# Decode attention with an MLP gate: one program loop over single units, with the small matrices behind the last one

## The chip, the cores and the metric

One core of a Trainium2 chip. The metric is the device time in microseconds of one execution. The engines are named as in the profile: PE multiplies matrices (PEld is its load of the stationary operand), DVE and ACT are the vector and scalar engines, POOL sets constants, SP issues nearly all DMA.

## The reference

Two sequences (B = 2), one new token each, width D = 512. The token is normalised and goes two ways: attention over a long cache, and an MLP whose SiLU gates the attention's output.

```python
xn = _layernorm(x)                                   # (2, 1, 512)
q = (xn @ wq)                                        # 32 heads of 128
k, v = repeat(k_cache, 4), repeat(v_cache, 4)        # caches: (2, 8, 32768, 128), bf16
p = softmax(q @ k * 128 ** -0.5)
s = (p @ v).reshape(2, 1, 4096) @ wo                 # (2, 1, 512)
h2 = gelu(_layernorm(xn + hs) @ w3) @ w4             # w3 (512, 1792), w4 (1792, 512)
g = silu(xn + hs + h2)
return x + s * g
```

With a sequence of length one the shifted parts that make up `hs` are all padding, so `hs` is zero, and w1 and w2 aren't read. What is read: 2 x 8 key caches and as many value caches of 8.39 MB each, wq and wo of 4.19 MB each, w3 and w4 of 1.84 MB each.

## The kernel before, in words

A **unit** n is one pair (sequence n % 2, cache head n // 2); there are 16. The four query heads that share a cache head are handled together.

*Buffers.* `vbuf` holds one whole value cache. `kbuf` has three places of half a key cache: a unit with n even has its keys in places 0 and 1, one with n odd in places 1 and 2, and each begins with the half in place 1 (`halves`). So the next unit's keys can be loaded as soon as the first half of this unit's has been turned.

*Scores.* DVE turns 128x2048 words of keys into one of two buffers `ktb` (`turned`, L378), eight times a unit; each turned block gives one group of eight matmuls of 128x512 (`scores`, L392) with the queries `qz` as stationary operand, whose columns ACT places anew for each unit (`place_q`). They fill `sc`, one of two PSUM tiles of 1024 columns.

*Softmax.* DVE takes the maximum of `sc` (L457); PE and DVE bring it across the partitions (L463 to L472); ACT makes the exponentials and their sums (L473); DVE turns them into `pT` (L476).

*Values.* 64 matmuls in four column strips of PE at a time add up `acc` (`v_job`, L490); DVE copies it out (`unit_copy`), and five small f32 matmuls, a reciprocal and a product give the unit's columns of `oQ` (`unit_end`).

*Order.* The order is written out by hand. A recorder (`Plan`) is told which regions each operation reads and writes and works out its semaphore waits; each engine then issues its operations in the order in which they were recorded. PE and DVE issue units 0 to 13 as a hardware loop of seven turns with two units each; ACT, POOL and SP have straight programs. `step(n)` interleaves two units: the first half of the scores of unit n+1, a part of its second half, the values of unit n, the rest of the scores, the softmax of n+1 and the end of n. SP issues the loads in the order K(n+1), V(n): the keys' load waits until DVE has turned a first half, the values' load until PE is through with `vbuf`.

*The start.* The queue begins with half of the first keys, wq, the other half, w3, w4; the three matrices lie in `vbuf`. `q_job` makes all queries with 128 matmuls (L430), and the MLP runs between the first unit's score groups (`mlp_in`, `mlp_gelu`, `mlp_out`, `mlp_gate`).

*The end.* The last unit's values come in three parts into `kbuf`, wo in four (`wo_cuts`, the last of two rows); `o_final` turns the attention's output, `wo_job` multiplies it with 128 narrow matmuls (L583), and DVE multiplies with the gate and adds x (L642, L643).

Of the kernel before, what the change touches and what calls it, by code (L numbers as in the profile page):

```python
# [7 lines left out]
F32 = mybir.dt.float32  # L8
# [7 lines left out]
GT = 16  # L16
# [4 lines left out]
class Op:  # L21
    def __init__(self, eng, fn, waits, done, turn, label):
        self.eng, self.fn, self.waits, self.done, self.turn, self.label = eng, fn, waits, done, turn, label


class Plan:

# [3 lines left out]
    def __init__(self, nc, sems):  # L33
        self.nc, self.sems = nc, sems
        self.engines = {
            "PE": nc.tensor, "DVE": nc.vector, "ACT": nc.scalar, "POOL": nc.gpsimd, "SP": nc.sync}
        self.count, self.hist, self.ops = {}, {}, {e: [] for e in self.engines}
        self.known = {e: {} for e in self.engines}
        self.after = {}
        self.turn = None  # L40

    def op(self, eng, fn, rd=(), wr=(), dma=None, label=None):
# [24 lines left out]
        self.count[sem] = self.count.get(sem, 0) + (16 if dma else 1)  # L67
# [13 lines left out]
        self.ops[eng].append(Op(eng, fn, waits, done, self.turn, label))  # L81

    def emit_one(self, o, waits):
        e = self.engines[o.eng]
        for s, v in waits:
            e.wait_ge(self.sems[s], v)  # L86
        o.fn().then_inc(self.sems[o.done[0]], 16 if o.done[0] != o.eng else 1)

    def emit_flat(self, eng):
        for o in self.ops[eng]:  # L90
            self.emit_one(o, sorted(o.waits.items()))

    def emit_looped(self, eng, kind):
# [7 lines left out]
        assert all(o.turn is not None for o in ops[first:last])  # L101
        plans, ahead = [], {}
        for k in range(body):
            same = [r[k] for r in rounds]
            assert len({o.label for o in same}) == 1
            line = {}
            for s in sorted({s for o in same[1:] for s in o.waits}):
                pts = [(i, o.waits[s]) for i, o in enumerate(same) if i and s in o.waits]
                step = self.step[s]
                base = pts[0][1] - pts[0][0] * step  # L110
                assert all(v == base + i * step for i, v in pts), (same[0].label, s, pts, step)
                assert base > 0, (same[0].label, s, base)
                line[s] = (base, step)
            for s, v in same[0].waits.items():
                if s not in line or line[s][0] < v:
                    ahead[s] = max(ahead.get(s, 0), v)
            plans.append(line)
# [3 lines left out]
        for s, v in sorted(ahead.items()):  # L121
            e.wait_ge(self.sems[s], v)
        with self.nc.Fori(0, len(rounds), 1, engines=[kind], hint_back_edge=True) as i:
            for o, line in zip(rounds[0], plans):
                self.emit_one(o, [(s, i * step + base) for s, (base, step) in line.items()])
# [5 lines left out]
def kernel(  # L131
# [37 lines left out]
    W3, W4 = DK * HD, DK * HD + DK * Fdim  # L169
    CW = UT * Dh  # L170
    assert NCH == 2 and NB == NS and NU % 2 == 0
# [5 lines left out]
    wo_cuts = [0, NR // 2, NR - 6, NR - 2, NR]  # L177

# [3 lines left out]
    def ps(name, words):  # L182
# [7 lines left out]
    ones_f = sb("ones_f", [128, 128], F32)  # L190
# [4 lines left out]
    qz = [sb(f"qz{b}", [128, 4, QW], BF16) for b in range(B)]  # L195
# [4 lines left out]
    sel = sb("sel", [128, 4, rep], F32)  # L200
    x_bf = sb("x_bf", [B, D], BF16)
    xf = sb("xf", [B, D], F32)
    xn = sb("xn", [B, D], F32)
    xT = sb("xT", [128, 2 * DK, B], BF16)
    q_sb = sb("q_sb", [128, B, Hq], BF16)
    oq = [sb(f"oq{b}", [128, rep], BF16) for b in range(B)]
# [4 lines left out]
    pT = [sb(f"pT{b}", [128, NHALF * GT, 32], BF16) for b in range(B)]  # L211
    acs = sb("acs", [128, 4 * Dh], F32)
# [5 lines left out]
    Sm = [sb(f"Sm{b}", [128, rep], F32) for b in range(B)]  # L218
    rc = sb("rc", [128, rep], F32)
    hf = sb("hf", [128, FK * B], F32)  # L220
    x2 = sb("x2", [128, FK * B], F32)
    th = sb("th", [128, FK * B], F32)
    h_bf = sb("h_bf", [128, FK * B], BF16)
    rows = {n: sb(n, [B, D], t) for n, t in (("xn_bf", BF16), ("ln2", F32), ("ln2_bf", BF16))}
# [5 lines left out]
    sc = [ps(f"sc{b}", NHALF * GT * 32) for b in range(B)]  # L230
    acc = ps("acc", 512)
    mi = [ps("mi0", 512), ps("mi1", 512)]
    s_ps = ps("s_ps", 512)[:, 0:128]

    sem_names = ["PE", "DVE", "ACT", "POOL", "k", "v", "k0", "k1", "wq", "w3", "w4", "x", "x4", "xn4",
                 "z0", "z1", "z2", "wo0", "wo1", "wo2", "wo3", "out0", "out1"]
# [6 lines left out]
    def dve(fn, rd=(), wr=(), label=None):  # L243
        P.op("DVE", fn, [al(r) if isinstance(r, str) else r for r in rd],
             [al(w) if isinstance(w, str) else w for w in wr], label=label)

    def act(fn, rd=(), wr=(), label=None):
        P.op("ACT", fn, [al(r) if isinstance(r, str) else r for r in rd],
             [al(w) if isinstance(w, str) else w for w in wr], label=label)

    def pool(fn, rd=(), wr=(), label=None):
        P.op("POOL", fn, [al(r) for r in rd], [al(w) for w in wr], label=label)

    def pe(fn, rd=(), wr=(), label=None):
        P.op("PE", fn, [al(r) if isinstance(r, str) else r for r in rd],
             [al(w) if isinstance(w, str) else w for w in wr], label=label)
# [18 lines left out]
    def load_k(n):  # L275
        c0 = place(n % 2, 0)
        load("k", kbuf[:, c0:c0 + NCH * CW], cache(A_k_cache, n), [kreg(c0, NCH * CW)])

    def load_k_half(n, c, sem):
        c0 = place(n % 2, c)  # L280
        load(sem, kbuf[:, c0:c0 + CW], cache(A_k_cache, n)[:, c * CW:(c + 1) * CW], [kreg(c0, CW)])
# [4 lines left out]
    def load_v_part(n, c, w0, w1, sem):  # L286
        load(sem, kbuf[:, c * CW + w0:c * CW + w1], cache(A_v_cache, n)[:, c * CW + w0:c * CW + w1],
             [kreg(c * CW + w0, w1 - w0)])

    def load_wo():  # L290
        for i, (r0, r1) in enumerate(zip(wo_cuts, wo_cuts[1:])):
            c0, c1 = 2 * CW + r0 * D, 2 * CW + r1 * D
            load(f"wo{i}", kbuf[:, c0:c1], wo_v[:, r0 * D:r1 * D], [kreg(c0, c1 - c0)])

    load_k_half(0, halves(0)[0], "k0")
    load("wq", vbuf[:, 0:DK * HD].rearrange("p (k f) -> p k f", k=DK), wq_v, [("vbuf", 0, W3)])
    load_k_half(0, halves(0)[1], "k1")
    load("w3", vbuf[:, W3:W3 + DK * Fdim].rearrange("p (k f) -> p k f", k=DK), w3_v, [("vbuf", W3, W4)])
    load("w4", vbuf[:, W4:W4 + FK * D].rearrange("p (f d) -> p f d", f=FK), w4_v,
         [("vbuf", W4, W4 + FK * D)])  # L300
# [9 lines left out]
    for b in range(B):  # L310
        pool(lambda b=b: G.memset(qz[b][:, :, :], 0.0), wr=[f"qz{b}"])
# [22 lines left out]
    xn_bf, ln2, ln2_bf = rows["xn_bf"], rows["ln2"], rows["ln2_bf"]  # L334
    dve(lambda: V.tensor_copy(out=xn_bf[:, :], in_=xn[:, :]), ["xn"], ["xn_bf"])
    dve(lambda: V.tensor_copy(out=identf[:, :], in_=ident[:, :]), ["ident"], ["identf"])
    layernorm(ln2, "ln2", xn, "xn", 2)
    dve(lambda: V.tensor_copy(out=ln2_bf[:, :], in_=ln2[:, :]), ["ln2"], ["ln2_bf"])

    treg = mi[0].bitcast(BF16)[:, 0:2 * DK * B]  # L340

    def transposes(j, src):
        def fn():
            sv = src[:, :].rearrange("b (p k) -> b k p", k=DK)
            for k in range(DK):
                r = T.transpose(
                    out=treg[:, (j * DK + k) * B:(j * DK + k + 1) * B],
                    in_=sv[:, k, :], identity=ident[0:B, 0:B])
            return r
        return fn  # L350

    pe(transposes(0, xn_bf), ["xn_bf", "ident"], ["mi0"])
    pe(transposes(1, ln2_bf), ["ln2_bf", "ident"], ["mi0"])
    dve(lambda: V.tensor_copy(out=xT[:, :, :], in_=treg.rearrange("p (k b) -> p k b", b=B)), ["mi0"], ["xT"])

    for k in range(4):
# [7 lines left out]
        ["identf"], ["headm"])  # L364
    sel2 = sel[:, :, :].rearrange("p i h -> p (i h)")
# [3 lines left out]
    dve(lambda: V.memset(acc[:, :], 0.0), [], ["acc"])  # L369
    dve(lambda: V.memset(s_ps, 0.0), [], ["s_ps"])  # L370

    waiting = []
    turns = [0]

    def turned(n, grp, c0):
        i = turns[0] % KTB
        turns[0] += 1
        dve(lambda: V.transpose(out=ktb[i][:, :], in_=kbuf[:, c0:c0 + KG * GT * Dh].bitcast(U32)),  # L378
            [kreg(c0, KG * GT * Dh)], [f"ktb{i}"], f"turn{n % 2}.{grp}")
        waiting.append((n, grp, i))  # L380

    def scores(n, grp, i):
        b = n % 2

        def fn():
            for x in range(KG):
                half, sl = (grp + x) // NS, (grp + x) % NS
                kv = ktb[i][:, x * GT * DW:(x + 1) * GT * DW].bitcast(BF16).rearrange(
# [298 lines left out]
```

## Time and profile before

| | |
|---|---|
| three runs | 657.02, 658.0 and 1265.22 us, median 658.0 |
| span of the profiled execution | 655.4 us, from its first to its last instruction |
| DMA | 280.64 MB, mean 428 GB/s |
| PE busy | 392.5 us (60%), 2637 matmuls |
| DVE busy | 359.8 us (55%) |
| ACT busy | 42.2 us (6%) |
| mean granted PE clock | 0.811 |

The profile is of one execution of its own; the record gives its span, and two of the three runs lie 1.6 and 2.6 us above it. The third run took nearly twice as long and has no profile. A line of the timeline gives start and length in microseconds, engine, line of the kernel, operation, what is written from what, the number of instructions, and in brackets how long the engine sat idle before it and what it waited for. A line of a stretch gives its bounds and length, then the busy time of PE, PEld, DVE, ACT and POOL, each with its count, then the granted PE clock, the DMA share and GB/s.

### The profile page before, as it was taken

The numbers are of one execution on the slowest core, as the hardware profiler recorded it, in microseconds if no ns is written. First come the engines' busy times: TensorE is split into PE (matmuls) and PEld (weight loads), VectorE is DVE, ScalarE is ACT, GpSimd is POOL, SyncE is SP. The second block draws the span as 40 slices with busy tenths as digits, with TensorE's granted clock in tenths as the row PEclk, the third lists the DMA queues.
The fourth block names the chain that finished last, engine by engine and source line by source line (L and its number), as shares of the span: only waits on it lengthen the run. The fifth ranks groups of instructions, "written<-read, shape, count | busy, mean of one in ns | idle before, by whom it ended". The sixth has DMA issues, their size and how long they took to land.

```text
span 655.4 us, 6232 instructions
## 1 busy us (share of the span) xinstructions
PE 392.5 (60%) x2637; PEld 167.1 (25%) x2637; DVE 359.8 (55%) x313; ACT 42.2 (6%) x124; POOL 2.5 (0%) x11
## 2 busy tenths in 40 slices
PE   0492756747385674738558474764837576472774
PEld 0341222222122222213222222221322223131233
DVE  6184827456482745738364572845558284564821
ACT  1102010000101000010100101010010101001000
POOL 1000000000000000000000000000000000000000
PEclk9986887868788685878968598796869879596987
DMA  9999999999999999999999999999999999999996
GB/s 382 415 453 436 445 428 420 437 440 448 408 444 432 444 432 420 440 436 444 428 428 436 440 444 412 444 432 444 428 424 440 436 444 428 428 432 441 420 419 275
DMA packets 6110, 280.64 MB, mean 428 GB/s; under 512 B 715, under 2 KB 725, under 8 KB 981
## 3 DMA queue, kind: packets, MB, share of 16 engines
q1 hardware_dynamic: 6056, 280.50, 99.0%
q8 instruction: 7, 0.11, 0.1%
q10 hardware_dynamic: 44, 0.01, 0.0%
q14 instruction: 3, 0.02, 0.0%
HBM read 280.50 MB, written 0.00 MB: 428 GB/s over the span
## 4 chain that ended last, share of the span: by engine, by line
DMA 71%; DVE 13%; PE 12%; issue 3%; ACT 0%; SPq 0%; DVEq 0%
DMA kbuf<-in_A_k_cache_dram 63%; DVE ktb L378 13%; PE sc L392 11%; DMA kbuf<-in_A_wo_dram 4%; DMA vbuf<-in_A_wq_dram 3%; PE mi L430 1%; PE s_ps L583 0%; ACT qz L420 0%; DVE qp L448 0%; PE mi L441 0%; SPq L260 0%; DVE sg L642 0%; DVE out_bf L643 0%; DVEq L86 0%; DVE q_sb L437 0%
## 5 line engine op out<-in xcount | busy, mean ns | idle before, releaser
L392 PE MATMUL sc<-ktb,qz 128*128 128x512 bf16 x1024 | 272.9, 419 | 162.3 <-DVE ktb L378 160.7
L378 DVE STREAM_TRANSPOSE ktb<-kbuf 128x2048 uint32<-128x2048 uint32 x128 | 285.3, 2283 | 108.9 <-DMA kbuf<-in_A_k_cache_dram 80.5
L392 PEld LDWEIGHTS sc<-ktb,qz 128*128 128x128 bf16 x1024 | 99.2, 104 | 328.2 <-DVE ktb L378 191.9
L490 PE MATMUL acc<-vbuf,pT 128*16 128x512 bf16 x960 | 69.3, 454 | 34.7 <-DMA vbuf<-in_A_v_cache_dram 34.7
L457 DVE TENSOR_REDUCE m<-sc 128x1 f32<-128x1024 f32 x16 | 19.6, 1225 | 125.1 <-PE sc L392 125.1
L490 PEld LDWEIGHTS acc<-vbuf,pT 128*16 128x16 bf16 x960 | 26.3, 103 | 77.6 <-DMA vbuf<-in_A_v_cache_dram 42.1
L420 ACT COPY qz<-qp 32x16 bf16<-32x16 bf16 x68 | 13.7, 202 | 481.2 <-PE sc L392 459.3
L476 DVE STREAM_TRANSPOSE pT<-pr 128x1024 bf16<-128x1024 bf16 x16 | 19.9, 1245 | 20.4 <-ACT pr L473 20.4
L473 ACT ACTIVATE pr<-sc,nb 128x1024 bf16<-128x1024 f32 x16 | 17.8, 1115 | 66.4 <-DVE nb L472 66.2
L510 PE MATMUL mi<-sel,acs 128*128 128x4 f32 x128 | 19.0, 272 | 0.0
L510 PEld LDWEIGHTS mi<-sel,acs 128*128 128x128 f32 x128 | 18.1, 218 | 0.0
L463 PE MATMUL mi<-identf,m 128*1 128x128 f32 x16 | 4.3, 270 | 20.4 <-DVE m L457 19.8
L501 DVE COPY acs<-acc 128x512 f32<-128x512 f32 x16 | 10.9, 682 | 6.7 <-PE acc L490 6.7
L469 PE MATMUL mi<-ones_f,gx 1*128 1x1 f32 x32 | 6.4, 268 | 13.0 <-DVE gx L467 13.0
L430 PE MATMUL mi<-xT,vbuf 128*128 128x2 bf16 x128 | 3.6, 165 | 14.3 <-DMA vbuf<-in_A_wq_dram 14.3
L469 PEld LDWEIGHTS mi<-ones_f,gx 1*128 1x128 f32 x32 | 5.1, 197 | 16.0 <-DVE gx L467 16.0
L463 PEld LDWEIGHTS mi<-identf,m 128*1 128x1 f32 x16 | 1.3, 79 | 28.0 <-DVE m L457 27.2
L508 PE MATMUL mi<-Sm,ones_f 128*128 128x4 f32 x32 | 6.8, 282 | 0.8 <-DVE acs L501 0.8
L490 PE MATMUL acc<-kbuf,pT 128*16 128x512 bf16 x64 | 5.2, 484 | 3.3 <-DMA kbuf<-in_A_v_cache_dram 1.7
L430 PEld LDWEIGHTS mi<-xT,vbuf 128*128 128x128 bf16 x128 | 3.5, 104 | 14.4 <-issue 14.4
L472 DVE TENSOR_SCALAR nb<-mi 128x1 f32<-128x1 f32 x16 | 2.5, 159 | 7.9 <-PE mi L469 7.9
L508 PEld LDWEIGHTS mi<-Sm,ones_f 128*128 128x128 f32 x32 | 5.4, 211 | 1.5 <-DVE acs L501 1.3
(73 smaller groups left out, 62.1 us busy)
## 6 DMA issues: line engine op xcount, KB each, us to landing
kbuf<-in_A_k_cache_dram SPq DMA_DIRECT2D x2, 4096.0 KB, 22.1
vbuf<-in_A_wq_dram SPq DMA_DIRECT2D x1, 4096.0 KB, 21.4
kbuf<-in_A_v_cache_dram SPq DMA_DIRECT2D x1, 4096.0 KB, 44.3
kbuf<-in_A_v_cache_dram SPq DMA_DIRECT2D x2, 2048.0 KB, 28.7
vbuf<-in_B_w_dram SPq DMA_DIRECT2D x2, 1792.0 KB, 37.4
kbuf<-in_A_wo_dram SPq DMA_DIRECT2D x1, 2048.0 KB, 28.6
kbuf<-in_A_wo_dram SPq DMA_DIRECT2D x1, 1280.0 KB, 27.2
kbuf<-in_A_wo_dram SPq DMA_DIRECT2D x1, 512.0 KB, 28.1
```

What stands on the lines that cost most here:

```text
L378: dve(lambda: V.transpose(out=ktb[i][:, :], in_=kbuf[:, c0:c0 + KG * GT * Dh].bitcast(U32)), [kreg(c0, KG * GT * Dh)], [f"ktb{i}"], f"turn ...
L392: r = T.matmul(sc[b][:, half * GT * 32:(half + 1) * GT * 32].rearrange("p (t k) -> p t k", k=32), lhsT=qz[b][:, k, off:off + 128], rhs=kv[ ...
L420: act(lambda i=i, c0=c0: A.copy(out=qz[b][32 * i:32 * i + 32, :, c0:c0 + rep], in_=qp[32 * i:32 * i + 32, :, b, g, :]), ["qp"], [(f"qz{b}" ...
L430: r = T.matmul(qT[:, h * B:(h + 1) * B], lhsT=vbuf[:, k * HD + h * Dh:k * HD + (h + 1) * Dh], rhs=xT[:, k, :], start=(k == 0), stop=(k == ...
L457: dve(lambda: V.tensor_reduce(out=m1[:, :], in_=sc[b][:, :], axis=AX.X, op=ALU.max), [f"sc{b}"], ["m1"], f"m{b}")
L469: pe(lambda: T.matmul(bc, lhsT=gx[:, :, :].rearrange("o x h -> o (x h)"), rhs=ones_f[0:1, 0:1], start=True, stop=True), ["gx", "ones_f"], ...
L473: act(lambda: A.activation(out=pr[:, :], in_=sc[b][:, :], func=ACT.Exp, bias=nb[:, 0:1], scale=inv_sqrt_dh, accum_out=S1[:, :]), [f"sc{b}" ...
L476: dve(lambda: V.transpose(out=pT[b][:, :, :].rearrange("p t r -> p (t r)"), in_=pr[:, :]), ["pr"], [f"pT{b}"], f"pT{b}")
L490: r = T.matmul(acc[32 * j:32 * j + 16, :].rearrange("p (i d) -> p i d", d=Dh), lhsT=pT[b][:, half * GT + u, r0:r0 + 16], rhs=vv[:, x - c0 ...
L501: dve(lambda: V.tensor_copy(out=acs[:, :], in_=acc[:, :]), ["acc"], ["acs"], f"acs{n % 2}")
L508: T.matmul(ot[:, rep:2 * rep], lhsT=ones_f[:, :], rhs=Sm[b][:, :], start=True, stop=True)
L510: r = T.matmul(ot[:, 0:rep], lhsT=acs[:, i * Dh:(i + 1) * Dh], rhs=sel[:, i, :], start=(i == 0), stop=(i == 3))
```

## The change

- **One unit at a time.** The loop's body is one unit on PE (16 turns) and two units on DVE (7 turns, the last two units behind it). A unit runs scores, softmax, values and end before the next one begins. There is one `sc`, one `qz` and one `pT` where there were two.
- **Loads.** SP issues wq, K(0), V(0), then K(n+1) and V(n+1) after the scores and the values of unit n. The last unit's keys come in two halves, its values in one piece. wq lies in place 2 of `kbuf`.
- **Loops on PE.** The scores are an inner loop of two turns (halves), whose output address in `sc` is worked out in a register; q is a loop of 16 turns with eight matmuls each, with addresses in registers.
- **End of a unit.** Instead of five f32 matmuls: DVE scales `acc` by the reciprocal of the sums and a mask (128x512), sums over its four blocks, and one small matmul and a copy on ACT write `oQ`. The sums over heads are one matmul (`headf`), ahead of the values.
- **Behind the last unit.** w3, w4 and wo are loaded behind the last values. The MLP works on rows: 16 matmuls of up to 512 columns, a gelu on 128x512 tiles (square and tanh on ACT), four turns on PE, 14 matmuls; 26 rows of wo go into four strips as wide matmuls, which a small f32 matmul gathers; the last six rows stay narrow.
- PE's program goes from 921 matmuls to 209.

```diff
-    load_k_half(0, halves(0)[0], "k0")
-    load("wq", vbuf[:, 0:DK * HD]..., wq_v, [("vbuf", 0, W3)])
-    load_k_half(0, halves(0)[1], "k1")
-    load("w3", ...)
-    load("w4", ...)
+    load("wq", wq_s, wq_v, [kreg(2 * CW, CW)])
+    load_k(0)
+    load_v(0)
...
+        def fn(done):
+            with nc.Fori(0, Hq // 2, 1, engines=[mybir.EngineType.PE]) as h2:
+                for e in range(2):
+                    for k in range(DK):
+                        r = T.matmul(
+                            qT[:, bass.ds(h2 * (2 * B) + e * B, B)],
+                            lhsT=kb[:, bass.ds(h2 * (2 * Dh) + (2 * CW + k * HD + e * Dh), Dh)],
+                            rhs=xT[:, k, :], start=(k == 0), stop=(k == DK - 1))
+                done(r)
...
+    def scores(n):
+        for h, c in enumerate(halves(n % 2)):
+            P.inner = h
+            for t in range(NB // KG):
+                i = t % KTB
+                c0 = place(n % 2, c) + t * KG * GT * Dh
+                dve(lambda i=i, c0=c0: V.transpose(
+                    out=ktb[i][:, :], in_=kbuf[:, c0:c0 + KG * GT * Dh].bitcast(U32)), ...)
+                def fn(un, hh, t=t, i=i):
+                    half = ((un + hh + 1) % 2) * HW
+                    for x in range(KG):
...
+                        for k in range(4):
+                            r = T.matmul(
+                                sc[:, bass.ds(half, HW)].rearrange("p (t k) -> p t k", k=32),
+                                lhsT=qz[:, k, off:off + 128], rhs=kv[:, k // 2, k % 2, :, :], ...)
+                pe(fn, [f"ktb{i}", "qz"], [("sc", c * HW, (c + 1) * HW)], f"sc{t}")
...
+    def unit_end(n):
+        b, g = n % 2, n // 2
+        ot = mA[:, 136:136 + rep]
+        dve(lambda: V.scalar_tensor_tensor(
+            out=acs[:, :, :], in0=acc[:, :].rearrange("p (i d) -> p i d", d=Dh), scalar=rS[:, 0:1],
+            in1=mask[:, :].unsqueeze(2).to_broadcast([128, 4, Dh]), op0=ALU.mult, op1=ALU.mult), ...)
+        dve(lambda: V.tensor_reduce(
+            out=acr[:, :], in_=acs[:, :, :].rearrange("p i d -> p d i"), axis=AX.X, op=ALU.add), ...)
+        pe(lambda: T.matmul(ot, lhsT=acr[:, :], rhs=headm[:, :], start=True, stop=True), ...)
+        act(lambda: A.copy(out=oQ[:, b, g * rep:(g + 1) * rep], in_=ot), ["mA"], [("oQ", n, n + 1)])
...
+    q_job()
+    place_q(0)
+    for n in range(NU):
+        P.turn = {"PE": n, "DVE": n // 2 if n < 2 * LOOP else None}
+        scores(n)
+        if n + 1 < NU:
+            load_k(n + 1)
+        softmax(n)
+        values(n)
+        if n + 1 < NU:
+            load_v(n + 1)
+        unit_end(n)
+    load("w3", w3_s, w3_v, [kreg(0, W4)])
+    load("w4", w4_s, w4_v, [kreg(W4, FK * D)])
+    for i, (r0, r1) in enumerate(zip(wo_cuts, wo_cuts[1:])):
+        load(f"wo{i}", kbuf[:, c0:c1], wo_v[:, r0 * D:r1 * D], [kreg(c0, c1 - c0)])
+    pe(mlp_in, [kreg(0, W4), "xT"], ["hP"])
...                                                  # oT, oP; square, tanh, four turns on PE
+    pe(mlp_out, [kreg(W4, FK * D), "h_bf"], ["mD"])
+    dve(lambda: V.tensor_copy(out=th[:, :], in_=mD[:, :]), ["mD"], ["th"])
+    wo_rows(wo_cuts[0], wo_cuts[1])
+    pe(gather(gP, th, True, True), ["sel", "th"], ["mA"])
...                                                  # the gate
+    wo_rows(wo_cuts[1], wo_cuts[2])
+    dve(lambda: V.tensor_copy(out=wsum[:, :], in_=wP[:, :]), ["wP"], ["wsum"])
+    wo_last(wo_cuts[2], wo_cuts[3])
+    pe(gather(s_ps, wsum, False, False), ["sel", "wsum"], ["s_ps"])
+    wo_last(wo_cuts[3], wo_cuts[4])
```

More of the change, by code (lines that the diff above doesn't have):

```diff
@@ new lines @@
+    steps = {}
+    for n in range(NU):
+        P.turn = {"PE": n, "DVE": n // 2 if n < 2 * LOOP else None}
+        before = dict(P.count)
+        scores(n)
[6 more added lines that the diff above has]
+        unit_end(n)
+        for s in ("PE", "DVE", "ACT"):
+            got = P.count[s] - before.get(s, 0)
+            assert n in (0, NU - 1) or steps.setdefault(s, got) == got, (s, n, got)
+    P.turn = {}
```

558 lines of the change are left out of this document (266 added, 292 removed).

## The prediction

> **What bounds the kernel now.** I read the page first (engines, DMA, queues), then the stretches of one pair of units, then one unit in order of time.
>
> ```profile
> span 655.4 us, 6232 instructions
> ...
> PE 392.5 (60%) x2637; PEld 167.1 (25%) x2637; DVE 359.8 (55%) x313; ACT 42.2 (6%) x124; POOL 2.5 (0%) x11
> ...
> DMA packets 6110, 280.64 MB, mean 428 GB/s; under 512 B 715, under 2 KB 725, under 8 KB 981
> ...
> q1 hardware_dynamic: 6056, 280.50, 99.0%
> q8 instruction: 7, 0.11, 0.1%
> ```
>
> No engine is busy for more than 60% of the span, while the queue that carries caches and weights fills 99.0% of what 16 DMA engines have. The stretches of two units (the columns after the engines are the granted clock, the DMA share and GB/s) say the same for the steady part:
>
> ```profile
> 61.70:100.40 38.70, 22.71 (x141) 9.34 (x141) 21.88 (x17) 2.21 (x7) 0.00 (x0) 0.81 1.00 434
> 100.40:139.00 38.60, 24.00 (x141) 9.64 (x141) 21.77 (x18) 2.21 (x7) 0.00 (x0) 0.81 1.01 435
> ```
>
> A unit is 38.6 us of DMA: 8.39 MB of keys and 8.39 MB of values, 19.3 us each at 434 GB/s. So the bytes set the time, and any order of the compute costs nothing as long as the DMA queue never runs dry and the work behind the last byte stays short. The change moves no byte: caches, wq, w3, w4 and wo are each read once, before and after. The question is only whether a load is issued too late, and what happens at the two ends.
>
> **One unit in order of time.** Picked rows of the unit whose keys land at 177.6, and behind them rows of other units for PE at a low clock (in the fourth from the end the values of another unit, then a stretch of it, where the granted clock is 0.50, then half of the values at that clock, then a group of scores at it):
>
> ```profile
> 177.61 4.50 DVE L378 STREAM_TRANSPOSE ktb<-kbuf 128x2048 uint32<-128x2048 uint32 x2 [4.74 <-DMA kbuf<-in_A_k_cache_dram]
> 179.97 7.98 PE L392 MATMUL sc<-ktb,qz 128*128 128x512 bf16 x24 [9.01 <-DVE ktb L378]
> 186.25 11.08 DVE L378 STREAM_TRANSPOSE ktb<-kbuf 128x2048 uint32<-128x2048 uint32 x5 [0.34 <-PE sc L392]
> 188.59 0.33 SPq L260 DMA_DIRECT2D kbuf<-in_A_k_cache_dram  x1
> 193.01 1.91 PE L392 MATMUL sc<-ktb,qz 128*128 128x512 bf16 x8 [0.28 <-DVE ktb L378]
> 196.92 3.63 PE L490 MATMUL acc<-vbuf,pT 128*16 128x512 bf16 x64 [2.00 <-DMA vbuf<-in_A_v_cache_dram]
> 200.60 0.33 SPq L260 DMA_DIRECT2D vbuf<-in_A_v_cache_dram  x1
> 204.17 1.23 DVE L457 TENSOR_REDUCE m<-sc 128x1 f32<-128x1024 f32 x1 [6.83 <-PE sc L392]
> 208.33 1.25 DVE L476 STREAM_TRANSPOSE pT<-pr 128x1024 bf16<-128x1024 bf16 x1 [1.27 <-ACT pr L473]
> 216.20 2.31 DVE L378 STREAM_TRANSPOSE ktb<-kbuf 128x2048 uint32<-128x2048 uint32 x1 [6.24 <-DMA kbuf<-in_A_k_cache_dram]
> 622.00 5.32 PE L490 MATMUL acc<-vbuf,pT 128*16 128x512 bf16 x64 [2.46 <-DMA vbuf<-in_A_v_cache_dram]
> 623.00:624.00 1.00, 1.00 (x16) 0.40 (x12) 0.00 (x0) 0.00 (x0) 0.00 (x0) 0.50 1.06 459
> 636.38 3.31 PE L490 MATMUL acc<-kbuf,pT 128*16 128x512 bf16 x32 [1.56 <-DVE pT L476]
> 141.37 3.37 PE sc L392 x8
> ```
>
> Write T for the moment the keys land. Eight turns on DVE end at T+19.7 (186.25 + 11.08 - 177.6); the first two score groups are slow on PE (3.37 for one at the low clock), the rest follow DVE. The last group takes 1.91 more: T+21.7. From the maximum to the turned probabilities is 5.4 (204.17 to 209.58). The values take 3.63 after a busy PE and 5.32 after an idle one, whose clock has fallen to 0.50; wholly at that clock they would take twice 3.31, 6.6. The next keys' load goes out at T+11.0, the next values' at T+23.0 (200.60), the moment PE is done with vbuf. The next keys land at T+38.6.
>
> **The change, part by part.**
>
> *Order of a unit.* Before, the values of unit n ran inside the scores of unit n+1, and the loads went K(n+1), V(n). Now a unit is finished before the next begins, and the loads go K(n), V(n), K(n+1). The sum from T: scores 21.7; softmax 5.4, so 27.1 (V(n) landed at T+19.3, it isn't waited for); values after PE sat nearly idle, 5.32: T+32.4. Then V(n+1) can be issued. DMA is then carrying K(n+1), which ends at T+38.6: the lead is 6.2 us, where it was 15.6 (38.6 - 23.0). K(n+1) goes out at T+11.0 as before, with V(n) under way until T+19.3: lead 8.3, as now. How much lead a load needs, the start shows:
>
> ```profile
> 0.95 0.39 SPq L260 DMA_DIRECT2D kbuf<-in_A_k_cache_dram  x1
> 1.00:2.00 1.00, 0.00 (x0) 0.00 (x0) 0.00 (x0) 0.00 (x0) 0.77 (x5) 1.00 0.61 166
> 2.00:3.00 1.00, 0.00 (x0) 0.00 (x0) 0.70 (x2) 0.00 (x0) 1.00 (x3) 1.00 1.31 360
> ```
>
> From the issue at 0.95 to full flow is 1 to 1.5 us (166 GB/s in the first microsecond, 360 in the next). 6.2 covers it with 4.7 to spare, so I cost the new order at nothing; if the unit became 6 us longer, each of 15 loads of values would leave about 1.3 us of empty queue. Behind the values stand two DVE passes over 128x512 (scaled copy, sum over four blocks), each bounded by the copy of acc below, 0.69, then a small matmul: DVE is free at T+33.9, 4.7 before the next keys. One score buffer, one qz and one pT in place of two add waits on work of the same unit that ends before T+34; nothing is queued behind them but the next turns, which wait for keys anyway.
>
> *Loops on PE.* Scores run in an inner loop over halves whose output address comes from a register, with one register instruction ahead of each group. PE waits 0.28 for DVE in each steady group (193.01 row), so a little work for the sequencer is hidden. The trace of before has no matmul with such an address: from below nothing, from above 3.4 a group, the slowest that one is seen. I take nothing, since the groups are limited by DVE at 2.2.
>
> *q looped.* 128 matmuls, with a register instruction before each (29 register operations in a turn of 8, in the program as built).
>
> ```profile
> 22.98 3.55 PE L430 MATMUL mi<-xT,vbuf 128*128 128x2 bf16 x128 [14.33 <-DMA vbuf<-in_A_wq_dram]
> 13.33 4.51 DVE L378 STREAM_TRANSPOSE ktb<-kbuf 128x2048 uint32<-128x2048 uint32 x2 [2.25 <-DMA kbuf<-in_A_k_cache_dram]
> 108.43 0.04 DVEq L86
> ```
>
> From below 3.55. From above 16 x 29 x 0.04 more (a register instruction of DVE's queue): 22. wq is now first in the queue, so it lands where the first 4.19 MB did, 13.3, and the first keys land 19.3 later, 32.6. Of this 19.3 the loop takes 3.6 to 22, nearer the lower end by count of instructions; the overrun of 3, and 2 more for q_sb, qp and qz, would come off a lead of 6.2. Cost: nothing, at most 1.
>
> *The end.* MLP and the whole of wo now stand behind the last unit.
>
> ```profile
> 602.68 4.51 DVE L378 STREAM_TRANSPOSE ktb<-kbuf 128x2048 uint32<-128x2048 uint32 x2 [6.36 <-DMA kbuf<-in_A_k_cache_dram]
> 643.38 0.69 DVE L501 COPY acs<-acc 128x512 f32<-128x512 f32 x1 [6.67 <-PE acc L490]
> 649.27 2.22 PE L583 MATMUL s_ps<-kbuf,oP 128*2 128x128 bf16 x64 [0.45 <-DMA kbuf<-in_A_wo_dram]
> 651.88 0.29 DVE L643 TENSOR_TENSOR out_bf<-sg,x 128x128 bf16<-128x128 f32 x1
> 4.77 0.53 DVE L326 TENSOR_SCALAR xn<-xf,mv,rstd 2x512 f32<-2x512 f32 x1
> 207.09 1.11 ACT L473 ACTIVATE pr<-sc,nb 128x1024 bf16<-128x1024 f32 x1 [2.04 <-DVE nb L472]
> 205.45 0.27 PE L463 MATMUL mi<-identf,m 128*1 128x128 f32 x1 [1.32 <-DVE m L457]
> 51.98 1.28 ACT L564 ACT_TABLE_LOAD   x1
> ```
>
> Before, behind the last keys (602.7) come 20.97 MB (two values, wo): 48.3 us, so the last byte is at 651.0, and the output is ready at 652.2, 3.2 before the span's end. Now 16.25 MB stand behind the last keys (values, w3, w4, wo: 37.4 us), which land at 613.6, their first half 9.7 earlier, 603.9; the last byte is at 651.0 again. But unit 14 holds DVE until 575.0 + 33.9 = 608.9. From there 19.7 + 1.9 + 5.4 + 5.3 give the end of the last values, 641.2 (639.3 if PE is still warm); I take 640.3. V landed at 632.9, so here compute is late, not DMA. Then one chain, with estimates from the rows above: two passes and the small matmul 1.7; 16 wide matmuls of the MLP 1.2 (a quarter of 64 in 3.63 to 5.32); square and tanh, half of the 1024-wide exponential's time, 0.65 each; two passes of 0.53 and two out of PSUM of 0.69; four PE turns and a copy 0.8; 14 wide matmuls 1.2; the first 16 rows of wo 1.3; a gather of four f32 matmuls 0.6 (0.27 for one, several at a time); ten rows 0.9; copy 0.7; gather 0.6; the last eight narrow ones 0.4; product and sum 0.6; and about twenty hand-overs of 0.05, 1.0. Together 14.7: ready at 655.0, 2.8 later than 652.2. Bounds: 1 us sooner if PE is warm throughout; 5 us later with the cold pace everywhere, slower f32 gathers and a table load of 1.28 in the chain.
>
> *The program's size.* PE's program falls from 921 matmuls to 209. What loading it costs can be seen in queue q8, 7 packets and 0.11 MB of 280.64 in all: nothing to gain. In the steady part there is no such packet at all (the list of queues from 216 to 564):
>
> ```profile
> ## 3 DMA queue, kind: packets, MB, share of 16 engines
> q1 hardware_dynamic: 2592, 151.00, 100.1%
> ```
>
> So the loop of 270 matmuls stayed in PE's memory over its turns, and the shorter one will too. The Trainium skill (Runtime: NRT & Kernel Launch, section Instruction fetch mechanics) holds against loops that a taken branch whose target lies outside the two pages at hand stalls until that page is fetched; by that rule the long loop should have fetched on each turn, and the time of the new one would be rival 2's; the trace bears out the other sum, with no fetch and nothing added.
>
> **Sum.** 655.4 + 0 (units) + 0 (q) + 2.8 (end) = 658.2 of span. The median of the runs, 658.0, is 2.6 above the profiled span; I carry that over: 660.8.
>
> **Rivals.**
> 1. *The values' load comes too late.* Place: SP's wait for PE ahead of each V(n+1). It decides from 37.3 after T on (38.6 less 1.3 to start). If PE kept the cold pace through a unit: 2.3 + 8 x 3.4 + 5.4 + 6.6 = 41.5, 4.2 over, fifteen times: 63 us, 724. At 2 us over it is 30: 691. For it: the lead shrinks to 6.2, and PE's first groups in each unit are cold today. Against: cold lasts 5 us in each burst and the sum already has it.
> 2. *Taken branches fetch code.* The mechanism would hold PE while a page of code waits behind large data packets: 5385 of 2 KB and more carry 280.6 MB, 52 KB each, 1.9 us at an engine's 27 GB/s, and as much again for the page. Two branches in a unit, up to 7 us, would use up the lead of 6.2 and leave 0 to 2 us of empty queue each: 661 to 690, most likely near 666. The quiet q8 speaks against it.
> 3. *The tail hides.* If the late MLP chain runs warm and its hand-overs overlap, or the last unit starts warm, the output is ready 0 to 1 later than before: 658 to 659; if the start also gets tighter, 656. Faster than that needs fewer bytes: 280.5 MB at 435 GB/s are 645 alone.
> 4. *It does nothing at all*, being a change of program size: 658.
>
> **How the numbers follow.** My forecast has 0.70 and reaches from 657 to 666, rivals 3 and 4 together 0.13, rival 2 0.04, rival 1 0.13. Rival 1 passes 2% (13 us, about what a measurement of this kernel can tell from no change) when it is over by 0.9 us a unit, for which I give 0.12. Faster by over 2% would mean under 645: 0.01. Within 2%: 0.87. The range takes in the tail's bounds, the hidden tail below and the beginning of rivals 1 and 2 above: 656 to 672.
>
> **What would show it.** Right: DMA share 1.00 and 434 GB/s in each unit, keys 38.6 apart, SP's issue of values 30 to 34 after the keys' landing, q8 with two or three packets, and DVE idle for some 4 us before each first turn for DMA. In the tail, PE waits for DVE and ACT, not for wo. Wrong: gaps of DMA each 38.6 us, the page's DMA row at 8, DVE turns over 2.3 apart with PE as releaser throughout, PEclk near 0.5 in the scores, or q's loop lasting past 33 us.

## The result, and the profile after

The changed kernel takes 667.29 us (median of five runs, 665.36 to 668.55) where the kernel before takes 658.0: a ratio of 1.0139 [1.0118, 1.0159], slower by 9.3 us by the medians, 1.4%. The profiled span is 665.5 against 655.4, 10.1 more. The forecast was 660.8, so it had the sign and about a third of the size; the time lies inside the range of 656 to 672, but above the 657 to 666 that the forecast gave to its own sum.

The page after:

```profile
span 665.5 us, 6187 instructions
PE 412.8 (62%) x2397; PEld 162.9 (24%) x2397; DVE 381.0 (57%) x304; ACT 41.3 (6%) x124; POOL 2.0 (0%) x11
q1 hardware_dynamic: 5768, 280.50, 97.7%
q8 instruction: 2, 0.03, 0.0%
```

The same 280.50 MB; the queue that carries them falls from 99.0% to 97.7% of what the 16 DMA engines have. The whole steady part, the keys of unit 2 to those of unit 14 (twelve units; columns as in the prediction's stretches, PE, PEld, DVE, ACT, POOL, clock, DMA share, GB/s):

```profile
112.90:577.20 464.30, 288.07 (x1620) 109.11 (x1620) 274.19 (x193) 26.06 (x84) 0.00 (x0) 0.83 1.00 434
```

464.30 / 12 = 38.7 a unit at 434 GB/s and a DMA share of 1.00, as before. From the first turn of unit 2's keys to that of unit 14's it is 464.25 (112.95 to 577.20), and 463.56 in the kernel before (100.41 to 563.97). So at most 0.7 was lost there, and nearly all of the 10.1 lies at the two ends. The start (timeline rows; SPq is SP's issue of a load), with the two stretches in which the queue ran short:

```profile
13.88 1.12 PE L428 MATMUL mA<-xT,kbuf 128*128 128x2 bf16 x8 [5.03 <-DVE mA L418]
37.12 1.11 PE L428 MATMUL mA<-xT,kbuf 128*128 128x2 bf16 x8 [0.44 <-issue]
39.98 4.47 DVE L465 STREAM_TRANSPOSE ktb<-kbuf 128x2048 uint32<-128x2048 uint32 x2
50.46 0.33 SPq L313 DMA_DIRECT2D kbuf<-in_A_k_cache_dram  x1
71.71 0.33 SPq L313 DMA_DIRECT2D vbuf<-in_A_v_cache_dram  x1
...
50.00:56.00 6.00, 5.16 (x23) 1.89 (x23) 6.00 (x4) 0.00 (x0) 0.00 (x0) 1.00 0.92 350
68.00:76.00 8.00, 4.11 (x59) 1.66 (x52) 4.25 (x4) 0.16 (x1) 0.00 (x0) 0.91 0.83 319
```

The q loop lasts from 13.88 to 38.23, 24.35 us: sixteen turns of 1.1 of work and 0.44 in which PE multiplies nothing. The first keys are turned only at 39.98, with no wait for DMA in the row: they had been there for a while. The next two loads go out late, and twice the queue runs dry for a moment: the DMA shares of 0.92 and 0.83 leave about 0.5 and 1.4 us. (A packet of 64 KB takes 2.4 us and is counted in the stretch in which it starts, so much shorter stretches say little.) By the starts and ends of the packets in the trace, the 16 DMA engines lost 0.4 us near 51 and 1.2 near 72, 1.6 in all. The end:

```profile
610.32 0.75 DVE L530 SCALAR_TENSOR_TENSOR acs<-acc,rS,mask 128x512 f32<-128x512 f32 x1 [5.93 <-PE acc L518]
611.11 1.02 DVE L534 TENSOR_REDUCE acr<-acs 128x128 f32<-128x512 f32 x1
638.46 5.80 PE L518 MATMUL acc<-vbuf,pT 128*16 128x512 bf16 x64 [0.77 <-DVE rS L507]
646.72 3.87 PE L574 MATMUL hP<-kbuf,xT 128*2 128x512 bf16 x16
655.20 1.87 PE L613 MATMUL mD<-kbuf,h_bf 128*2 128x512 bf16 x14 [0.27 <-DVE h_bf L606]
656.44 2.33 PE L631 MATMUL wP<-kbuf,oP 128*2 128x512 bf16 x16
661.97 0.29 DVE L663 TENSOR_TENSOR out_bf<-sg,x 128x128 bf16<-128x128 f32 x1
...
652.00:654.00 2.00, 0.00 (x0) 0.00 (x0) 1.27 (x3) 1.53 (x2) 0.00 (x0) 0.79 0.46 180
653.00:654.00 1.00, 0.00 (x0) 0.00 (x0) 0.85 (x2) 0.98 (x2) 0.00 (x0) 0.57 0.03 10
654.00:656.00 2.00, 1.41 (x12) 0.58 (x16) 0.44 (x2) 0.38 (x1) 0.00 (x0) 0.50 0.03 8
```

The last bytes land near 653 (180 GB/s in 652 to 654, 8 in the next 2 us), the output is ready at 662.26: 9 us of compute behind the last byte, where before there was 1.1. No wait for wo stands in these rows; the MLP's first product alone takes 3.87.

### The profile page after: what moved, and what is told of

It reads as the page before. It is cut to its first block, busy times and chain, and to the rows that moved or that the text cites. A ratio compares the mean times of both kernels' runs of the same rounds, so it can differ in the third digit from the quotient of the medians.

```text
span 665.5 us, 6187 instructions
## 1 busy us (share of the span) xinstructions
PE 412.8 (62%) x2397; PEld 162.9 (24%) x2397; DVE 381.0 (57%) x304; ACT 41.3 (6%) x124; POOL 2.0 (0%) x11
## 3 DMA queue, kind: packets, MB, share of 16 engines
q1 hardware_dynamic: 5768, 280.50, 97.7%
HBM read 280.50 MB, written 0.00 MB: 421 GB/s over the span
## 4 chain that ended last, share of the span: by engine, by line
DMA 55%; PE 19%; DVE 18%; issue 6%; ACT 1%; another core or an unknown queue 1%; DVEq 0%; ACTq 0%; SPq 0%
DMA kbuf<-in_A_k_cache_dram 55%; DVE ktb L465 14%; PE sc L477 12%; PE mA L428 3%; PE acc L518 2%; DVE m L490 1%; ACT pr L500 1%; PE wP L631 0%; DVE pT L506 0%; DVE acs L530 0%; DVE acr L534 0%; PE mD L613 0%; DMA x_bf<-in_A_x_dram 0%; DVE stats L366 0%
## 5 line engine op out<-in xcount | busy, mean ns | idle before, releaser
L518 PE MATMUL acc<-vbuf,pT 128*16 128x512 bf16 x1024 | 86.4, 512 | 13.7 <-DVE rS L507 13.7
L530 DVE SCALAR_TENSOR_TENSOR acs<-acc,rS,mask 128x512 f32<-128x512 f32 x16 | 12.0, 751 | 88.7 <-PE acc L518 88.7
L537 PE MATMUL mA<-headm,acr 128*128 128x4 f32 x32 | 6.3, 268 | 30.7 <-DVE acr L534 30.7
L428 PE MATMUL mA<-xT,kbuf 128*128 128x2 bf16 x128 | 17.7, 183 | 11.7 <-issue 6.7
L503 PE MATMUL mA<-S,headf 128*128 128x1 f32 x32 | 7.9, 318 | 23.8 <-ACT pr L500 23.8
L428 PEld LDWEIGHTS mA<-xT,kbuf 128*128 x128 | 13.3, 104 | 16.1 <-issue 13.1
L534 DVE TENSOR_REDUCE acr<-acs 128x128 f32<-128x512 f32 x16 | 16.3, 1018 | 0.6
L537 PEld LDWEIGHTS mA<-headm,acr 128*128 128x128 f32 x32 | 4.9, 194 | 38.8 <-DVE acr L534 38.8
L503 PEld LDWEIGHTS mA<-S,headf 128*128 128x128 f32 x32 | 6.6, 257 | 25.2 <-ACT pr L500 25.2
L496 PE MATMUL mA<-ones_f,gx 1*128 1x1 f32 x32 | 6.5, 268 | 9.9 <-DVE gx L494 9.9
```

The costliest lines, as they stand in the source:

```text
L428: r = T.matmul(qT[:, bass.ds(h2 * (2 * B) + e * B, B)], lhsT=kb[:, bass.ds(h2 * (2 * Dh) + (2 * CW + k * HD + e * Dh), Dh)], rhs=xT[:, k, ...
L503: pe(lambda: T.matmul(sS, lhsT=headf[:, :, :].rearrange("p x h -> p (x h)"), rhs=S1[:, :], start=True, stop=True), ["headf", "S1"], [rO], "S")
L518: r = T.matmul(acc[32 * j:32 * j + 16, :].rearrange("p (i d) -> p i d", d=Dh), lhsT=pT[:, half * GT + u, r0:r0 + 16], rhs=vv[:, x, u, :, : ...
L530: dve(lambda: V.scalar_tensor_tensor(out=acs[:, :, :], in0=acc[:, :].rearrange("p (i d) -> p i d", d=Dh), scalar=rS[:, 0:1], in1=mask[:, : ...
L534: dve(lambda: V.tensor_reduce(out=acr[:, :], in_=acs[:, :, :].rearrange("p i d -> p d i"), axis=AX.X, op=ALU.add), ["acs"], ["acr"], "acr")
L537: pe(lambda: T.matmul(ot, lhsT=acr[:, :], rhs=headm[:, :], start=True, stop=True), ["acr", "headm"], ["mA"], "ot")
```

## The experiments

The theory after this reading: about 2 of the 10 us are the q loop's, because matmuls with addresses in registers follow each other slowly, and about 8 are the end's, where MLP and wo form one chain of compute; the single units cost nothing. Its rivals: the loop itself (its turns) and not its addresses; single units that cost something hidden in the average; and an end that waits for bytes and not for compute.

### The start: is it the loop, and what in it?

**q written out**, the rest as after:

```diff
-            with nc.Fori(0, Hq // 2, 1, engines=[mybir.EngineType.PE]) as h2:
-                ... (addresses from h2)
+            for h in range(Hq):
+                for k in range(DK):
+                    c = 2 * CW + k * HD + h * Dh
+                    r = T.matmul(qT[:, h * B:(h + 1) * B], lhsT=kb[:, c:c + Dh], ...)
```

> q's 128 matmuls are written out with fixed addresses; all else as changed. Theory of the two ends: q ends by about 18 instead of 38.2, the first turn of keys starts when the first keys land (33 instead of 40.0), no queue gap near 53 and 71, all later keys land 2.2 us sooner, and the output too: span 663.3 (665.5 less 2.2), ratio to before 1.010 to 1.011. Rival (the serial order of units starves the queue in every unit): the start is a detail, the keys' spacing stays above 38.6 and the span stays within 0.7 of 665.5. Rival (the tail alone sets the end by its own loads): same, no change.

Measured: 663.93, ratio 1.0094 [1.0077, 1.0111], span 663.8: the ratio a little under the expected one, the span 0.5 above it.

```profile
13.55 3.57 PE L428 MATMUL mA<-xT,kbuf 128*128 128x2 bf16 x128 [4.71 <-DVE mA L418]
33.97 4.51 DVE L463 STREAM_TRANSPOSE ktb<-kbuf 128x2048 uint32<-128x2048 uint32 x2 [15.01 <-DMA kbuf<-in_A_k_cache_dram]
660.23 0.29 DVE L661 TENSOR_TENSOR out_bf<-sg,x 128x128 bf16<-128x128 f32 x1
```

The same 128 matmuls take 3.57, DVE waits for the first keys again, and unit 14's keys land at 575.01 instead of 577.20. The packets of this trace leave no gap at the start. In the profiles the output is 1.7 sooner, not 2.2, by the medians the kernel is 3.4 faster; so the loop's price is known as 2 to 3 us and no better. The output is still 8.35 later than before (660.52 against 652.17), which can only be the end.

**The loop kept, its addresses fixed** (every turn computes the same two heads):

```diff
-                            qT[:, bass.ds(h2 * (2 * B) + e * B, B)],
-                            lhsT=kb[:, bass.ds(h2 * (2 * Dh) + (2 * CW + k * HD + e * Dh), Dh)],
+                            qT[:, e * B:(e + 1) * B],
+                            lhsT=kb[:, 2 * CW + k * HD + e * Dh:2 * CW + k * HD + (e + 1) * Dh],
```

> The loop of q keeps its 16 turns of eight matmuls, but with fixed addresses (each turn makes the same two heads again, so q and the output are not the reference's). Which part of the 1.54 us of a turn is it? If the registers are the price (an operation of 0.046 ahead of each matmul and an address that PE must fetch): a turn takes the 0.22 of eight matmuls written out plus the 0.44 of the loop's end, 0.66, q 10.6 in all, no gap near 53, keys as with q written out. If the turn itself is (PE drains before it branches): 1.1 to 1.5 a turn, 18 to 24 in all.

Measured: one time of 661.74, span 660.0.

```profile
13.64 6.25 PE L428 MATMUL mA<-xT,kbuf 128*128 128x2 bf16 x128 [4.79 <-DVE mA L418]
32.67 4.50 DVE L465 STREAM_TRANSPOSE ktb<-kbuf 128x2048 uint32<-128x2048 uint32 x2 [10.94 <-DMA kbuf<-in_A_k_cache_dram]
```

6.25 for sixteen turns, 49 ns a matmul, less than either side expected: a turn costs 0.17 by itself ((6.25 - 3.57) / 16), and the registers are the price. With them the loop spends 24.35 / 128 = 190 ns on a matmul, written out 28. The source view of the line (ns, lowest, median, highest; first two lines the changed kernel, the last with q written out) shows that the matmul itself is not the difference:

```profile
L428 PEldq FUSED_REGOPS  x128: 42/46/79, 13.8 to 37.9; - x128
L428 PE MATMUL mA<-xT,kbuf x128: 181/184/185, 13.9 to 38.0; 128*128 128x2 bf16 x128
L428 PE MATMUL mA<-xT,kbuf x128: 165/165/187, 13.6 to 17.0; 128*128 128x2 bf16 x128
```

One matmul takes 184 with registers and 165 without. Written out they overlap, and one starts every 28 ns. With a register operation of 46 ns ahead of each, eight of them take 1.11, so one starts about every 130 ns ((1.11 - 0.18) / 7), and 0.44 follow before the next turn. Whether the address of the output or that of the weights costs more was not tried.

**The kernel before, with its q looped** in the same way (fifteen turns, the last pair written out):

```diff
-            for h in range(Hq):
+            with nc.Fori(0, Hq // 2 - 1, 1, engines=[mybir.EngineType.PE]) as h2:
+                ... (as in the changed kernel)
+            for h in range(Hq - 2, Hq):
```

> The kernel before, with q looped over 15 pairs of heads as in the change (the last pair written out); nothing left out. There, wq lands at 22.9 and the first keys wait for q, not the other way round. If the loop's price is the same and only its cover differs: q ends at 46 to 48 instead of 26.5, the second keys' load goes out 20 later, at 56 to 57, the queue runs dry after w4 (39) for 17 to 19 us, span 672 to 675. If the 24 us came from something else at the start of the changed kernel: q under 10 us, span 655 to 660.

Measured: one time of 676.2, span 674.4, 19.0 above the span of the kernel before, as expected.

```profile
23.29 1.12 PE L432 MATMUL mi<-xT,vbuf 128*128 128x2 bf16 x8 [14.64 <-DMA vbuf<-in_A_wq_dram]
44.88 1.10 PE L432 MATMUL mi<-xT,vbuf 128*128 128x2 bf16 x8 [0.43 <-issue]
56.72 0.33 SPq L260 DMA_DIRECT2D kbuf<-in_A_k_cache_dram  x1
50.00:54.00 4.00, 4.00 (x14) 1.36 (x11) 1.81 (x1) 0.70 (x1) 0.00 (x0) 1.00 0.00 0
```

The same loop costs 19.0 here and 2 to 3 there. In the kernel before nothing covers it: wq is in only at 23, the first half of the keys is there by then, and the queue stands at 0 GB/s (no packet of a load from 40.7 to 57.7). The changed kernel brings wq first, and 19.3 us of keys run over the loop. The cover is what the new order gives, and the loop uses it up.

### The end: bytes or compute, and which compute?

**w3 read in rows**: the hidden columns are taken in the order in which they lie, so that the moving operand is contiguous instead of every 14th element; w4 is left as it is, so hidden columns and rows of w4 no longer match.

```diff
-        w3 = w3_s.rearrange("p k (q f) -> p k f q", f=FK)
+        w3 = w3_s.rearrange("p k (f q) -> p k f q", f=FK)
```

> The 16 matmuls of the MLP's first layer read w3's columns in the order in which they lie, 256 bytes at a stretch, instead of every 14th; this permutes the hidden columns, so the output isn't the reference's. If the stride makes them slow: 1.7 instead of 3.9 us, the span 2.0 to 2.2 shorter (663.4). If the low PE clock alone makes them slow (it is 0.50 for most of them): still 3.3 to 3.9, span 665 to 665.5.

Measured: 665.48, ratio 1.0122 [1.0105, 1.0139], span 662.6. By medians 1.8 sooner than after, by the spans 2.9. The first row is of this run; the other two, of the run with q written out, have the strided product of the changed kernel at a full clock.

```profile
646.84 1.03 PE L574 MATMUL hP<-kbuf,xT 128*2 128x512 bf16 x16
645.04 3.81 PE L572 MATMUL hP<-kbuf,xT 128*2 128x512 bf16 x16
645.00:649.00 4.00, 3.98 (x18) 0.55 (x18) 0.25 (x1) 0.27 (x2) 0.00 (x0) 1.00 0.97 403
```

The sixteen matmuls take 1.03 instead of 3.87. The granted clock differs between these two: 1.00 with the rows, 0.57 on average from 646 to 650 in the changed kernel. But the strided product took 3.81 at 1.00 too, so the clock is not the reason: the stride of 28 bytes is the whole excess over the 1.2 of the forecast. The Trainium skill (Advanced Engine Details and Errata, SBUF Cachelines) says that reads run at full performance where subsequent accesses hit the same line of 16 bytes, and at a penalty where each access is to another line. With a step of 28 bytes each element lies on another line, and the pair 3.81 and 1.03 agrees.

**No MLP**: its loads are kept, its arithmetic is left out (mlp_in, gelu, the turns, mlp_out and their gather; the gate is made of xn alone).

```diff
-    pe(mlp_in, [kreg(0, W4), "xT"], ["hP"])
-    ... (gelu, h_turn, mlp_out, gather)
+    dve(lambda: V.tensor_add(out=t4[:, :], in0=xn4[:, :], in1=xn4[:, :]), ...)
```

> Leaves out the MLP's arithmetic (both matmuls, the gelu and the gather): the gate is made from the normalised token alone, so the output isn't the reference's; w3 and w4 are still loaded. Theory of the two ends: wo's rows can start when the last unit's output is turned, about 648, and then run into the last bytes (653): output 654 to 656 instead of 662.3, span 657.5 to 659.5. Rival (the last bytes of DMA set the end, 653, and what is behind it is only wo): less than 2 us are gained, span over 663.5.

Measured: 661.59, ratio 1.0056 [1.0039, 1.0073], span 660.6: above the expected range, by 1.1 by the span.

```profile
652.71 1.45 PE L610 MATMUL wP<-kbuf,oP 128*2 128x512 bf16 x10 [1.07 <-DMA kbuf<-in_A_wo_dram]
655.41 0.60 PE L621 MATMUL s_ps<-kbuf,oP 128*2 128x128 bf16 x16 [1.25 <-DMA kbuf<-in_A_wo_dram]
657.02 0.29 DVE L639 TENSOR_TENSOR out_bf<-sg,x 128x128 bf16<-128x128 f32 x1
```

Without the MLP, PE does wait for wo, and the output comes 2 us after its last part. So the MLP's compute was worth 5 us of the changed kernel's end (662.26 against 657.31), and below that the bytes rule. That they came 1 to 1.5 later than in the changed kernel is why the expectation was too low, and the MLP has no part in it: unit 2's keys were already 1.4 late (114.34 against 112.95). The q loop of this execution left the queue dry for longer: the loads behind it went out at 51.18 and 73.25, and by the packets the engines lost 3.2 us where the changed kernel's profile has 1.6.

**MLP early**: w3 is loaded ahead of the last values, its product stands in the gap of the last softmax, gelu runs beside the last values, mlp_out behind the unit's last matmul; PE's last unit is written out behind the loop.

```diff
+        if n + 1 == NU:
+            pe(mlp_in, [kreg(0, W4), "xT"], ["hP"])      # behind "bc" of the last softmax
...
+        if n + 1 == NU:
+            gelu(); pe(h_turn, ...)                      # behind the last values
...
+            pe(mlp_out, [kreg(W4, FK * D), "h_bf"], ["mD"])
```

> w3 is loaded ahead of the last unit's values instead of behind them, the first layer of the MLP stands in the softmax of the last unit on PE, the gelu beside its values, the second layer behind its last small matmul; PE's last unit stands behind the loop. Nothing is left out. Theory of the two ends: the gelu's chain (650.6 to 654.3) and the first layer (3.9) leave the end; the values come 4.2 us later from DMA (w3 ahead of them) and so start 0 to 1 later; output ready 655 to 657 instead of 662.3, span 658 to 660, ratio 1.003 to 1.006. Rival (end set by DMA's last bytes): no more than 1 to 2 gained.

Measured: 661.08, ratio 1.0053 [1.0036, 1.007], span 659.3. Ratio and span lie where they were expected.

```profile
634.46 3.82 PE L491 MATMUL hP<-kbuf,xT 128*2 128x512 bf16 x16
640.79 5.27 PE L549 MATMUL acc<-vbuf,pT 128*16 128x512 bf16 x64 [2.19 <-DMA vbuf<-in_A_v_cache_dram]
648.29 1.03 PE L500 MATMUL mD<-kbuf,h_bf 128*2 128x512 bf16 x14
652.96 0.81 PE L641 MATMUL wP<-kbuf,oP 128*2 128x512 bf16 x10 [1.70 <-DMA kbuf<-in_A_wo_dram]
655.75 0.29 DVE L672 TENSOR_TENSOR out_bf<-sg,x 128x128 bf16<-128x128 f32 x1
```

The strided product is as dear as ever (3.82), but it now stands where PE had nothing to do. Values and wo wait for bytes again, and the output is ready at 656.04, 6.2 sooner than after: the order of the end, not its amount, was the price.

### The units: how much lead does a load need?

The sum put the values' load 6.2 us ahead of the queue's end and called 1.3 enough. Values run twice or three times take lead away without moving a byte (each pass begins the sums anew, so they come out the same):

```diff
-            for x in range(nx):
+            for x in [x for _ in range(2) for x in range(nx)]:      # 3 in the other kernel
```

> The values' 64 matmuls of each unit are issued twice, the second pass beginning anew: the unit's chain is 3.7 longer, the values' load goes out at T+36.6 instead of T+33, a lead of 2.0. By the forecast's rule (1.3 is enough) the steady units stay 38.6 apart; 3.7 are added at the start, where the second values are already late, and 3.7 at the end: span 671 to 674. By the rival (a load needs its lead of over 2): each unit is 0.5 to 1.5 longer, 39.1 to 40.1 apart, span 680 to 695.

Measured: one time of 687.84, span 686.1, in the rival's range.

```profile
310.72 0.33 SPq L313 DMA_DIRECT2D vbuf<-in_A_v_cache_dram  x1
313.71 4.50 DVE L465 STREAM_TRANSPOSE ktb<-kbuf 128x2048 uint32<-128x2048 uint32 x2 [1.18 <-DMA kbuf<-in_A_k_cache_dram]
348.81 0.33 SPq L313 DMA_DIRECT2D vbuf<-in_A_v_cache_dram  x1
354.22 4.50 DVE L465 STREAM_TRANSPOSE ktb<-kbuf 128x2048 uint32<-128x2048 uint32 x2 [3.60 <-DMA kbuf<-in_A_k_cache_dram]
392.98 4.50 DVE L465 STREAM_TRANSPOSE ktb<-kbuf 128x2048 uint32<-128x2048 uint32 x2 [1.51 <-DMA kbuf<-in_A_k_cache_dram]
```

The lead is read here from the issue of the values to the first turn of the keys ahead of them. Values issued 2.99 ahead of the keys (310.72, 313.71) are followed by 40.51 to the next keys; issued 5.41 ahead (348.81, 354.22) by 38.76. The ten such pairs from 191 to 551, sorted:

| lead, us | 5.41 | 5.16 | 4.31 | 4.22 | 3.98 | 3.51 | 3.33 | 2.99 | 2.74 | 2.27 |
|---|---|---|---|---|---|---|---|---|---|---|
| to the next keys | 38.76 | 38.89 | 38.73 | 38.79 | 38.98 | 39.21 | 40.35 | 40.51 | 39.67 | 40.67 |

From about 4 up a load costs at most 0.4, below 3.4 it costs 1 to 2 us. The changed kernel's leads, read in the same way from twelve units, are 4.98 to 7.41, and its intervals 38.6 to 38.9: the steady units were safe, with 1 to 3 to spare, not 4.7.

> The same three times: the values' load goes out at T+40.3, 1.7 after the keys before it have landed. By the forecast's rival 1 (too late from T+37.3 on) each unit is 3.0 longer, 41.6 apart: 14 units 42, 7.4 at each end, span about 722. If compute were already the bound of a unit, it would be 48 or more apart, 800; if loads could overlap what follows, under 690.

Measured: one time of 715.7, span 713.9.

```profile
326.07 4.49 DVE L465 STREAM_TRANSPOSE ktb<-kbuf 128x2048 uint32<-128x2048 uint32 x2
352.49 12.75 PE L518 MATMUL acc<-vbuf,pT 128*16 128x512 bf16 x192 [0.77 <-DVE rS L507]
367.02 4.49 DVE L465 STREAM_TRANSPOSE ktb<-kbuf 128x2048 uint32<-128x2048 uint32 x2
```

A unit takes 40.95 (326.07 to 367.02), and DVE no longer waits for keys: here the chain of compute has become the bound, so this run is close to rival 1's figure without its mechanism.

### Both ends undone, the rest of the change kept

**MLP early and q written out**, with nothing left out:

> Both repairs together: q written out, and the MLP moved ahead of and beside the last unit's values; the order of single units, the scores' inner loop and all of wo at the end stay. Nothing left out. Theory of the two ends: the repairs add up (2.2 at the start, 6 at the end), the last bytes land at 650.5 to 651 as before the change, the rows of wo wait for them, the output is ready about 2 later: 652.5 to 653.5, span 656 to 657, ratio 1.000 to 1.003. Rival (single units cost something of their own in each unit): a rest of 3 us or more stays, ratio 1.005 or more.

Measured: 658.19 (657.38 to 658.47), ratio 1.0012 [1.0003, 1.0021], span 656.7. As expected.

```profile
649.71 1.45 PE L639 MATMUL wP<-kbuf,oP 128*2 128x512 bf16 x10 [0.64 <-DMA kbuf<-in_A_wo_dram]
653.13 0.29 DVE L670 TENSOR_TENSOR out_bf<-sg,x 128x128 bf16<-128x128 f32 x1
650.00:652.00 2.00, 1.64 (x30) 0.54 (x26) 0.79 (x2) 0.00 (x0) 0.00 (x0) 0.50 0.13 46
```

The output is ready at 653.42, 1.25 after that of the kernel before, with PE waiting for the bytes of wo. Single units, one score buffer, the scores' loop over halves, the new unit end and wo behind the last unit cost a tenth of a per cent together, the early MLP included. No version tried beats the kernel before.

Four kernels now form a square: q looped or written out, the MLP late or early. Their ratios are 1.0139, 1.0094, 1.0053 and 1.0012. Writing q out gains 0.45% with the MLP late and 0.41% with it early, 2.7 to 3.0 us; moving the MLP gains 0.86% and 0.82%, 5.4 to 5.7 us (each difference is good to some 0.2%). The two prices add up and leave 0.8 us.

## Why the prediction was right in its sign and wrong in its size

Two terms of the sum were too small. The q loop stood at nothing, at most 1, and cost 2 to 3 us. The chain behind the last values stood at 14.7 and took 18.0, with smaller excesses ahead of it. So the output came 10.1 later than in the kernel before (662.26 against 652.17), not 2.8.

*Order of a unit: right, its rule wrong.* Values were issued 31 to 34 after the keys' landing, keys came 38.6 to 38.9 apart, and the cost was at most 0.7 over twelve units. But "from the issue to full flow is 1 to 1.5 us" was read at an empty queue; behind a full one a load needs about 4 (values twice). Rival 1 therefore decides from about T+34.6 on, not T+37.3.

*Loops on PE: right for the scores, wrong for q.* For q even the upper bound of 22 was too low. That it came near 24.35 is luck: it added 29 register operations of 0.04 a turn to matmuls 28 ns apart, where the source view has eight of 0.046 on the line, matmuls about 130 ns apart and 0.44 at the end of each turn. The value taken, near the lower end "by count of instructions", had no row under it. The loop lasted to 38.2; past 33 was one of the prediction's own signs of being wrong. The first keys were then turned 7.3 late (39.98 against 32.67 with fixed addresses), the second keys' load went out at 50.46 with the queue due to end near 52, a lead of 1.5: the "lead of 6.2" was gone, and 2.2 were lost where the sum had nothing, at most 1 (577.20 against 575.01 with q written out; with the loop at fixed addresses they land at 573.68, so 3.5 against that; of this 1.3 is there at the first keys, which came at 33.97 with q written out and at 32.67 with fixed addresses).

*The end: the mechanism right, its size wrong.* The last byte stayed near its place (about 653 against 651) and compute was late, as the sum said. From its 655.0 to the measured 662.26 are 7.3; without the start's 2.2 that is 5.1, just past the prediction's bound of 5 for a cold end. The terms differ as follows (measured by the rows of the end above; the values' forecast is what the sum took, 640.3 less 635.9):

| term of the sum | forecast | measured | difference |
|---|---|---|---|
| keys of unit 14 land | 575.0 | 577.20 | +2.2 |
| unit 14 holds DVE from then | 33.9 | 34.9 | +1.0 |
| scores and softmax of the last unit | 27.0 | 26.3 | -0.7 |
| its values | 4.4 | 5.80 | +1.4 |
| the chain behind them | 14.7 | 18.0 | +3.3 |

Three causes of the last row were measured. The two DVE passes take 0.75 and 1.02, where the copy of acc had given 0.69 for each. "16 wide matmuls of the MLP 1.2" were 3.87, since their operand is strided; in rows they take 1.03, so the count was right and the shape of the read was overlooked. And PE is cold, that is, at half its clock: it does nothing from 650.72 to 654.32 while gelu runs, the granted clock is 0.57 from 653 to 654 and 0.50 behind it, so that 16 rows of wo took 2.33 instead of 1.3 and mlp_out 1.87 instead of 1.2. With the MLP early, the same 14 matmuls of mlp_out took 1.03 at a clock of 1.00. The Trainium skill (TensorE: Matmul & The Clock Gate, What's actually happening) has the clock fall to half after an idle window of about 3.4 us. Here it fell at about 653.1, some 2.4 after PE's last product, so sooner than a whole idle window. Together the three make 4.8 where the row has 3.3, since the rest of the chain was shorter than its terms: PE began the rows of wo 0.63 before mlp_out was through, for one. The values, too, began at a clock of 0.50 (638 to 642). The bound of 5 later named this cold pace; the value taken did not hold it. The forecast should have asked whether each term of a serial chain has a row of its own shape, and none of these had.

*Program size: right.* q8 carried 2 packets, no gain and no fetch. That by the cited rule the long loop should have fetched on each turn was read too strictly: the rule is about targets outside what PE has at hand, and no run here shows how much that is. Rival 2 (taken branches fetch code) is out: with the two ends undone, the loops of single units cost 0.1%. Rivals 3 and 4 fell with the end.

## What to carry to other kernels

Where DMA is the bound, an order of compute that keeps the queue's lead was free here, and what a change costs is read at the two ends, where no bytes cover the work. Count a serial tail by rows of the same shape, stride and clock, and move its parts into the gaps of the last covered unit before trimming them. A small job put into a loop was cheap as long as its addresses stayed fixed; with addresses in registers it needs cover for its whole length.

## What the runs showed of the hardware

- 128 matmuls of 128x128 by 128x2 took 3.57 us written out (one every 28 ns), 6.25 in a loop of sixteen turns with fixed addresses and 24.35 with addresses from registers. A single one took 165 to 184 ns in all three: the registers cost the overlap of the matmuls and a longer end of each turn.
- A moving operand with a step of 28 bytes made 16 matmuls of up to 512 columns take 3.81 us at a clock of 1.00 and 3.87 at about 0.6; contiguous they took 1.03 at 1.00.
- 14 matmuls of 512 contiguous columns took 1.03 us at a clock of 1.00 and 1.87 at 0.50.
- In a busy queue, a load issued about 4 us or more before the keys ahead of it were turned cost at most 0.4, one issued less than 3.4 before cost 1 to 2.
